# A dynamic convolution fused with a tanh-shrink MLP: softmax one superblock further ahead, three first products on GpSimd

## The chip, the cores and the metric

The kernel runs on one core of a Trainium2 chip. The metric is the device time of one execution in microseconds (us). Several executions are timed and their median is the time of the kernel. One further execution is taken with the hardware profiler, and every line of a profile below comes from such an execution. Times inside it count from the start of its span.

## The reference

```python
# x (8, 4096, 192), weight_gen (8, 4096, 8 heads, 7 taps)
w = exp(weight_gen - max); w = w / (sum(w, taps) + 1e-9)
out[b,s,h,g] = sum_k w[b,s,h,k] * x_pad[b, s+k, h*24+g]     # six rows of zeros ahead
h = out.reshape(32768, 192) @ w_in          # 192 -> 2048
y = (h - tanh(h)) @ w_out                   # 2048 -> 192, float32
```

Each token has its own softmax over seven taps for each of eight heads; the softmax weights multiply the token's row of x and the six rows before it. The result passes through two matmuls with `h - tanh(h)` between them.

## The kernel before

**Tiling.** The 32768 tokens are cut into 32 superblocks of 1024 tokens (`TOK`), numbered n. A partition holds eight neighbouring tokens. The 192 channels are cut into three chunks of 64 (`NC`), the 2048 hidden columns into sixteen f tiles of 128. Every PE operand uses 64 rows, and two row halves (r = 0, 1) stand side by side in the array.

**The stages of one superblock.**

- `load(n)` (L80) puts two transfers on SP's queue: `wg_t` with the weights (L84, 224 KB) and `x_t` with the rows of x (L93, 1344 KB; for the first superblock of a sequence a zero fill and three pieces, L103, L107, L93).
- `softmax_exp(n)` (L119) is one Exp on ACT.
- `softmax_norm(n)` (L129) is three instructions on DVE: the sum (`zsum`, L132), the reciprocal (L137), and the multiplication that gives `wsm` (L147). The reciprocal is written to the upper columns of a PSUM bank, here a bank of the second matmul (`obank`) or of the transposes (`pc`).
- `products(n)` (L153) multiplies the seven shifted copies of x with their tap's weight, 1536 elements a partition each, on GpSimd (POOL), except for the first two superblocks, where DVE takes some (`on_vector`). From superblock 3 on, a DMA adds the odd products onto the even ones (L179).
- `conv(n)` (L195) transposes the products on PE against an identity and sums them in PSUM (L213); ACT copies the sum to `convT` (L223).
- `gemm1(n, f)` (L240) is twelve half-array matmuls for two f tiles, six for one (L245), a Tanh on ACT (`th`, L255) and a subtraction on DVE (`gt`, L257).
- `gemm2(i)` (L264) is the second matmul for one block of 128 tokens (L277). Call i does the first half (r = 0) of block i and the second half of block i-1, in turns, in the banks `obank0` and `obank1`; ACT then copies block i-1 out (L295).

**The order.** The schedule is written out by hand (L362 to L403), and each engine runs its instructions in that order. The main loop runs over n, and inside it p runs from 0 to 7: two `gemm1` calls, from n = 1 on one `gemm2` call for the superblock before, and at fixed p the softmax of superblock n+3 and the transposes of superblock n+1. `products(n + 2)` is issued at the start of iteration n.

**What limits the queues.** The pool of `wg_t`, `e_t` and `wsm` has two buffers each, that of `x_t` two, that of the products two, and three PSUM buffers (`psum_h`) go round among `ph` and `pc`. So `gemm1` of f tile k waits until the `gt` of tile k-3 is done. The x of superblock n+3 can be loaded only when the products of superblock n+1 are finished on POOL.

**The start.** The weights w_in are loaded and cast by GpSimd's DMA queue in two parts: f tiles 0 to 5 (`load_w_in(0, FA)`) and the rest (`rest_of_w_in`, issued by the hook after product k = 2 of superblock 0). The upper 64 partitions get a copy of the lower ones, the first part on ACT's queue and the rest on SP's (L357). f tile 6 of superblock 0 needs that second copy.

Of the kernel before, what the change touches and what calls it, by code (L numbers as in the profile page):

```python
# [8 lines left out]
FP32 = mybir.dt.float32  # L9
BF16 = mybir.dt.bfloat16  # L10

ACT = mybir.ActivationFunctionType
# [4 lines left out]
def kernel(  # L17
# [8 lines left out]
    nc = tc.nc  # L26
# [24 lines left out]
    const = ctx.enter_context(tc.tile_pool(name="const", bufs=1))  # L51
    xpool = ctx.enter_context(tc.tile_pool(name="xpool", bufs=2))
    wgpool = ctx.enter_context(tc.tile_pool(name="wgpool", bufs=2))
    ppool = ctx.enter_context(tc.tile_pool(name="ppool", bufs=2))
    cpool = ctx.enter_context(tc.tile_pool(name="cpool", bufs=2))
    tpool = ctx.enter_context(tc.tile_pool(name="tpool", bufs=3))
# [20 lines left out]
    g1_act = {}  # L77
    last_wsm = {}

    def load(n):  # L80
        b, s = divmod(n, NSB)
        s0 = s * TOK
        wg_t = wgpool.tile([P, J, H, K], FP32, name="wg_t")
        nc.sync.dma_start(  # L84
            out=wg_t[:],
            in_=weight_gen[b, s0 : s0 + TOK].rearrange("(p j) h k -> p j h k", p=P),
        )

        x_t = xpool.tile([P, HALO + J, D], FP32, name="x_t")

        def rows(p0, p1):
            win = x[b, s0 + p0 * J - HALO : s0 + p0 * J - HALO + 1]
            nc.sync.dma_start(  # L93
                out=x_t[p0:p1, :, :],
                in_=bass.AP(
                    tensor=win.tensor,
                    offset=win.offset,
                    ap=[[J * D, p1 - p0], [D, HALO + J], [1, D]],
                ),
            )  # L100

        if s == 0:
            nc.sync.dma_start(  # L103
                out=x_t[0:1, 0:HALO, :],
                in_=zero[:].rearrange("o (h d) -> o h d", h=1).to_broadcast([1, HALO, D]),
            )
            nc.sync.dma_start(  # L107
                out=x_t[0:1, HALO : HALO + J, :],
                in_=x[b, 0:J].rearrange("(p j) d -> p j d", p=1),
            )  # L110

            rows(1, 16)
            rows(16, P)
        else:
            rows(0, P)
        wg_of[n] = wg_t
        x_of[n] = x_t

    def softmax_exp(n):  # L119
# [6 lines left out]
        )  # L126
        e_of[n] = e_t

    def softmax_norm(n, bank, in_psum=False):  # L129
        e_t = e_of.pop(n)  # L130
        zsum = wgpool.tile([P, J * H], FP32, name="zsum")
        nc.vector.reduce_sum(  # L132
            out=zsum[:], in_=e_t[:].rearrange("p j h k -> p (j h) k"), axis=AX.X
        )

        zr = bank[:, 512 - J * H : 512]
        nc.vector.reciprocal(zr, zsum[:])  # L137
        wsm_v = None
        if in_psum:
            wsm_v = obank[n % 2][:, 0 : J * H * K].rearrange("p (j h k) -> p j h k", j=J, h=H)  # L140
            scale(wsm_v, e_t, zr)
        wsm = wgpool.tile([P, J, H, K], FP32, name="wsm")
        last_wsm[0] = scale(wsm[:], e_t, zr)
        wsm_of[n] = (wsm, wsm_v)

    def scale(wsm, e_t, zr):
        return nc.vector.tensor_mul(  # L147
            wsm.rearrange("p j h k -> p (j h) k"),
            e_t[:].rearrange("p j h k -> p (j h) k"),
            zr.rearrange("p (n o) -> p n o", o=1).to_broadcast([P, J * H, K]),  # L150
        )

    def products(n, on_vector=(), hooks={}):  # L153
        x_t = x_of.pop(n)
        wsm, wsm_v = wsm_of.pop(n)
        in_pairs = n not in PLAIN

        even = ppool.tile([P, NPAIR, NC, J, H, GC], BF16, name="even")
        odd = ppool.tile([P, NPAIR, NC, J, H, GC], BF16, name="odd")
        last = ppool.tile([P, NC, J, H, GC], BF16, name="last")  # L160
        dst = {}
        for i in range(NPAIR):
            dst[2 * i] = even[:, i]
            dst[2 * i + 1] = odd[:, i]
        dst[K - 1] = last[:]
        if -1 in hooks:
            hooks[-1]()
        for k in range(K):
            eng, w = (nc.vector, wsm_v) if k in on_vector else (nc.gpsimd, wsm[:])
            eng.tensor_mul(  # L170
                dst[k].rearrange("p c j h g -> p j h c g"),
                x_t[:, k : k + J, :].rearrange("p j (h c g) -> p j h c g", h=H, c=NC),
                w[:, :, :, k : k + 1]
                .rearrange("p j h (k o) -> p j h k o", o=1)
                .to_broadcast([P, J, H, NC, GC]),
            )
            if k == K - 2 and in_pairs:

                nc.gpsimd.dma_start(  # L179
                    out=even[:].rearrange("p i c j h g -> p (i c j h g)")[:, 0:ACC],  # L180
                    in_=odd[:].rearrange("p i c j h g -> p (i c j h g)")[:, 0:ACC],
                    accum_op=mybir.AluOpType.add,
                    max_dma_last_dim=4096,
                )
            if k in hooks:
                hooks[k]()
        if in_pairs:
            groups = [even[:, i] for i in range(NPAIR)] + [last[:]]
            prods_of[n] = [
                groups + ([odd[:, NPAIR - 1]] if c == NC - 1 else []) for c in range(NC)  # L190
            ]
        else:
            prods_of[n] = [[dst[k] for k in sorted(range(K), key=lambda k: k in on_vector)]] * NC

    def conv(n, chunks):  # L195

        prods = prods_of[n]
        if n not in conv_of:
            conv_of[n] = cpool.tile([P, NC, HT], BF16, name="convT")
        convT = conv_of[n]  # L200
        nch = len(chunks)
        pc = psum_h.tile([P, 2, HT], FP32, name="pc", tag="ph")
        steps = [
            (gi, ci, c)
            for gi in range(max(len(prods[c]) for c in chunks))
            for ci, c in enumerate(chunks)
            if gi < len(prods[c])
        ]
        for si, (gi, ci, c) in enumerate(steps):
            for j in range(JH):  # L210
                col = (ci * JH + j) * R
                for r in range(2):
                    nc.tensor.matmul(  # L213
                        pc[:, r, col : col + R],
                        lhsT=prods[c][gi][r * R : (r + 1) * R, c, 2 * j : 2 * j + 2].rearrange(
                            "p j h g -> p (j h g)"
                        ),
                        rhs=ident[r * R : (r + 1) * R, r * R : (r + 1) * R],
                        start=(si == 0 and j == 0),
                        stop=(si == len(steps) - 1 and j == JH - 1),  # L220
                    )
        c0 = chunks[0]
        nc.scalar.activation(  # L223
            out=convT[:, c0 : c0 + nch, :].rearrange("p c (j r t) -> p r (c j) t", r=2, t=R),
            in_=pc[:, :, 0 : nch * JH * R].rearrange("p r (cj t) -> p r cj t", t=R),
            func=ACT.Copy,
        )
        if c0 + nch == NC:
            prods_of.pop(n)
        return pc[:, 0]  # L230

    def order(inst, other, reason):
        tc.add_manual_dep(
# [122 lines left out]
    def copy_w_in(f0, f1, eng):  # L356
        eng.dma_start(out=w_in[R:P, :, f0:f1], in_=w_in[0:R, :, f0:f1])  # L357
# [1 line left out]
    def rest_of_w_in():  # L359
        load_w_in(FA, F)  # L360

    load(0)  # L362
    softmax_exp(0)
    softmax_norm(0, obank[0], in_psum=True)
    load(1)
    load_w_in(0, FA)
    products(0, on_vector=(1, 3, 4, 5, 6), hooks={2: rest_of_w_in})
    softmax_exp(1)
    softmax_norm(1, obank[1], in_psum=True)
    copy_w_in(0, FA, nc.scalar)  # L370
    copy_w_in(FA, F, nc.sync)
    products(1, on_vector=(0, 1), hooks={4: load_w_out})
    conv(0, (0, 1))
    conv(0, (2,))
    load(2)
    for n in range(NTOT):
        if n + 3 < NTOT:
            load(n + 3)
        if 1 <= n < NTOT - 2:
            products(n + 2)  # L380
        for p in range(J):
            gemm1(n, 2 * p)
            gemm1(n, 2 * p + 1)
            if n == 0 and p == 1:
                softmax_exp(2)
            if p == 5 and n + 3 < NTOT:
                softmax_exp(n + 3)
            if n >= 1:
                gemm2((n - 1) * J + p)
            if n + 1 < NTOT:  # L390
                if p == (6 if n > 0 else 7):
                    conv(n + 1, (0, 1))
                if p == (6 if n > 1 else 7):
                    bank = conv(n + 1, (2,))
            if n == 0 and p == 1:
                softmax_norm(2, obank[0])
                products(2)
            if p == 6 and n + 3 < NTOT:

                softmax_norm(n + 3, bank if n > 1 else obank[0])  # L400
    gemm2(LAST)
    for j in range(J):
        gemm2_last(j)  # L403
# [30 lines left out]
```

The softmax here doesn't subtract the row's maximum and nothing guards it: scores larger than these inputs give would overflow.

## Time and profile before

| | us |
|---|---|
| median of 3 runs | 781.7 |
| lowest, highest | 778.25, 781.99 |
| the profiled execution | 779.38 |
| its span, first to last instruction | 777.4 |

| stage (from the timeline) | begins at us |
|---|---|
| `gemm1` of superblock 0 | 20.27 |
| transposes of superblock 1 | 43.97 |
| `gemm1` of superblock 1 | 48.08 |
| transposes of superblock 2 | 67.06 |
| transposes of superblock 3 | 91.78 |
| transposes of superblock 4 | 114.60 |
| transposes of superblock 5 | 137.42 |

The profiled execution's own time is 1.98 us above its span, and 2.32 us under the median. From superblock 3 on, one superblock takes 22.8 us in most iterations. The groups of instructions give the length of each operation: a `gt` on DVE 1.219 us, a Tanh on ACT 1.022, a product on POOL 2.962, an Exp 0.577, and the three instructions of a softmax on DVE 0.610, 0.561 and 0.622.

### The profile page before, as it was taken

The numbers are of one execution on the slowest core, as the hardware profiler recorded it, in microseconds if no ns is written. First come the engines' busy times: TensorE is split into PE (matmuls) and PEld (weight loads), VectorE is DVE, ScalarE is ACT, GpSimd is POOL, SyncE is SP. The second block draws the span as 40 slices with busy tenths as digits, with TensorE's granted clock in tenths as the row PEclk, the third lists the DMA queues.
The fourth block names the chain that finished last, engine by engine and source line by source line (L and its number), as shares of the span: only waits on it lengthen the run. The fifth ranks groups of instructions, "written<-read, shape, count | busy, mean of one in ns | idle before, by whom it ended". The sixth has DMA issues, their size and how long they took to land.

```text
span 777.4 us, 32332 instructions
## 1 busy us (share of the span) xinstructions
PE 742.6 (96%) x14784; PEld 582.8 (75%) x14784; DVE 671.3 (86%) x626; ACT 640.7 (82%) x865; POOL 664.4 (85%) x259
## 2 busy tenths in 40 slices
PE   2689999999999999999999999999999999999997
PEld 1257777777777778777777787777877777777777
DVE  6988898889889888989889898888898989888883
ACT  1678888888888888888888888888888888888883
POOL 5999999999989998999989989999899999998000
PEclk9899999999999999999999999999999999999999
DMA  7814676766545666454566544576544566633112
GB/s 203 201 63 106 160 180 179 178 167 158 118 141 140 180 180 178 89 141 144 169 180 160 137 119 146 159 180 180 155 87 150 149 180 179 167 78 77 44 43 83
DMA packets 25849, 111.38 MB, mean 143 GB/s; under 512 B 4801, under 2 KB 9841, under 8 KB 21625
## 3 DMA queue, kind: packets, MB, share of 16 engines
q1 hardware_dynamic: 14688, 77.04, 28.0%
q0 software_dynamic: 10816, 31.99, 25.2%
q8 instruction: 115, 1.88, 1.0%
q10 hardware_dynamic: 208, 0.29, 0.2%
q14 instruction: 22, 0.17, 0.1%
HBM read 54.49 MB, written 25.17 MB: 102 GB/s over the span
## 4 chain that ended last, share of the span: by engine, by line
PE 92%; DVE 2%; DMA 2%; issue 1%; ACT 1%; POOL 1%; SPq 0%; DVEq 0%; POOLq 0%
PE ph L245 43%; PE obank L277 42%; PE pc L213 6%; DVE gt L257 2%; PE po L311 1%; DMA w_in<-in_moe_w_in_dram 1%; DMA x_t<-in_x_dram 1%; DMA wg_t<-in_weight_gen_dram 1%; ACT th L255 1%; POOL even L170 1%; DVE wsm L147 0%; DVE obank L137 0%; DVE zsum L132 0%; POOL w_in L346 0%; SPq L103 0%
## 5 line engine op out<-in xcount | busy, mean ns | idle before, releaser
L257 DVE TENSOR_TENSOR gt<-ph,th 128x1024 bf16<-128x1024 f32 x512 | 602.8, 1219 | 68.7 <-ACT th L255 66.7
L255 ACT ACTIVATE th<-ph 128x1024 f32<-128x1024 f32 x512 | 497.0, 1022 | 68.2 <-PE ph L245 68.0
L245 PE MATMUL ph<-convT,w_in 64*128 64x512 bf16 x3072 | 388.8, 378 | 11.0 <-DVE gt L257 8.3
L277 PEld LDWEIGHTS <-gt 64*128 64x128 bf16 x7936 | 347.2, 94 | 52.6 <-issue 3.8
L277 PE MATMUL obank<-w_out,gt 64*128 64x192 bf16 x7936 | 376.8, 243 | 3.1 <-issue 1.8
L170 POOL TENSOR_TENSOR even<-x_t,wsm 128x1536 bf16<-128x1536 f32 x94 | 278.4, 2962 | 36.6 <-PE ph L245 29.6
L170 POOL TENSOR_TENSOR odd<-x_t,wsm 128x1536 bf16<-128x1536 f32 x92 | 272.5, 2962 | 0.0
L245 PEld LDWEIGHTS <-w_in 64*128 64x128 bf16 x3072 | 179.7, 94 | 120.3 <-issue 26.7
L170 POOL TENSOR_TENSOR last<-x_t,wsm 128x1536 bf16<-128x1536 f32 x31 | 103.4, 3337 | 0.0
L295 ACT ACTIVATE out_sb<-obank 128x192 f32<-128x192 f32 x248 | 82.2, 331 | 16.6 <-PE obank L277 11.5
L223 ACT ACTIVATE convT<-pc 128x1024 bf16<-128x1024 f32 x64 | 48.7, 808 | 30.1 <-PE pc L213 30.1
L213 PE MATMUL pc<-ident,even 64*128 64x64 bf16 x2304 | 48.3, 191 | 16.6 <-POOL even L170 15.1
L213 PEld LDWEIGHTS <-even 64*128 64x128 bf16 x2304 | 43.1, 96 | 17.3 <-POOL even L170 15.3
L179 POOL DMA_DIRECT2D even<-odd x29 | 34.9, 1205 | 9.0 <-POOL odd L170 9.0
L137 DVE RECIPROCAL pc<-zsum 128x64 f32<-128x64 f32 x27 | 15.1, 561 | 13.7 <-ACT convT L223 13.7
L122 ACT ACTIVATE e_t<-wg_t 128x448 f32<-128x448 f32 x32 | 18.5, 577 | 9.7 <-DMA wg_t<-in_weight_gen_dram 9.7
L213 PE MATMUL pc<-ident,last 64*128 64x64 bf16 x768 | 23.5, 191 | 0.3 <-DVE last L170 0.3
L132 DVE TENSOR_REDUCE zsum<-e_t 128x64 f32<-128x448 f32 x32 | 19.5, 610 | 4.1 <-ACT e_t L122 4.1
L147 DVE TENSOR_TENSOR wsm<-e_t,pc 128x448 f32<-128x448 f32 x27 | 16.8, 622 | 2.8
L213 PEld LDWEIGHTS <-last 64*128 64x128 bf16 x768 | 17.3, 96 | 0.4 <-DVE last L170 0.4
L213 PE MATMUL pc<-ident,odd 64*128 64x64 bf16 x448 | 15.6, 198 | 0.0
L213 PEld LDWEIGHTS <-odd 64*128 64x128 bf16 x448 | 11.5, 100 | 0.0
(20 smaller groups left out, 54.0 us busy)
## 6 DMA issues: line engine op xcount, KB each, us to landing
x_t<-in_x_dram SPq DMA_DIRECT2D x24, 1344.0 KB
even<-odd POOLq DMA_DIRECT2D x29, 1024.0 KB, 9.1
out_dram<-out_sb SPq DMA_DIRECT2D x31, 768.0 KB
x_t<-in_x_dram SPq DMA_DIRECT2D x8, 1176.0 KB
wg_t<-in_weight_gen_dram SPq DMA_DIRECT2D x32, 224.0 KB
x_t<-in_x_dram SPq DMA_DIRECT2D x8, 157.5 KB
w_out<-in_moe_w_out_dram POOLq DMA_DIRECT2D x1, 768.0 KB, 10.0
out_dram<-out_sb SPq DMA_DIRECT2D x4, 192.0 KB
```

Of the source, the lines that this page charges most:

```text
L122: nc.scalar.activation(out=e_t[:].rearrange("p j h k -> p (j h k)"), in_=wg_t[:].rearrange("p j h k -> p (j h k)"), func=ACT.Exp,)
L132: nc.vector.reduce_sum(out=zsum[:], in_=e_t[:].rearrange("p j h k -> p (j h) k"), axis=AX.X)
L147: return nc.vector.tensor_mul(wsm.rearrange("p j h k -> p (j h) k"), e_t[:].rearrange("p j h k -> p (j h) k"), zr.rearrange("p (n o) -> p ...
L170: eng.tensor_mul(dst[k].rearrange("p c j h g -> p j h c g"), x_t[:, k : k + J, :].rearrange("p j (h c g) -> p j h c g", h=H, c=NC), w[:, : ...
L179: nc.gpsimd.dma_start(out=even[:].rearrange("p i c j h g -> p (i c j h g)")[:, 0:ACC], in_=odd[:].rearrange("p i c j h g -> p (i c j h g)" ...
L213: nc.tensor.matmul(pc[:, r, col : col + R], lhsT=prods[c][gi][r * R : (r + 1) * R, c, 2 * j : 2 * j + 2].rearrange("p j h g -> p (j h g)") ...
L223: nc.scalar.activation(out=convT[:, c0 : c0 + nch, :].rearrange("p c (j r t) -> p r (c j) t", r=2, t=R), in_=pc[:, :, 0 : nch * JH * R].re ...
L245: nc.tensor.matmul(ph[:, r, :], lhsT=w_in[r * R : (r + 1) * R, c, f * P : (f + 1) * P], rhs=convT[r * R : (r + 1) * R, c, :], start=(c == ...
L255: last_act[0] = nc.scalar.activation(out=th[:], in_=ph_f, func=ACT.Tanh)
L257: nc.vector.tensor_sub(gt[:], ph_f, th[:])
L277: mm = nc.tensor.matmul(po[:, 0:D], lhsT=g_of[n][f][r * R : (r + 1) * R, col : col + P], rhs=w_out[r * R : (r + 1) * R, f, :], start=(r == ...
L295: last_act[0] = nc.scalar.activation(out=out_sb[:, j, :], in_=po[:, 0:D], func=ACT.Copy)
```

## The change

There are four parts.

1. The weights get their own load function (`load_wg`), and in the loop they are loaded for superblock n+4 instead of n+3, behind the x of superblock n+3. `wsm` moves to a pool of its own with three buffers. `softmax_exp` and `softmax_norm` run for superblock n+4 in iterations n >= 1. To get one superblock ahead, iteration 1 does two softmaxes: superblock 4 at p = 1 (Exp) and p = 2 (DVE), and superblock 5 at p = 5 and p = 7.
2. The weights of superblocks 2 and 3 are loaded before the second copy of w_in on SP's queue.
3. Of superblock 0, product k = 1 goes from DVE to GpSimd, which then does k = 0, 1, 2. The hook that loads the rest of w_in still stands after k = 2.
4. The last multiplication of superblock 2's softmax moves from DVE to GpSimd (`softmax_norm_gpsimd`), its place from p = 1 to p = 2. The transposes of superblock 0 are issued product by product over all three chunks, in the order 3, 0, 4, 5, 1, 6, 2, instead of chunks 0 and 1 first and then chunk 2.

```diff
+    wpool = ctx.enter_context(tc.tile_pool(name="wpool", bufs=3))
...
-    def load(n):
+    def load_wg(n):
         b, s = divmod(n, NSB)
         s0 = s * TOK
         wg_t = wgpool.tile([P, J, H, K], FP32, name="wg_t")
...
+        wg_of[n] = wg_t
+
+    def load_x(n):
+        b, s = divmod(n, NSB)
+        s0 = s * TOK
...
-    def softmax_norm(n, bank, in_psum=False):
+    def softmax_sum(n):
         e_t = e_of.pop(n)
         zsum = wgpool.tile([P, J * H], FP32, name="zsum")
         nc.vector.reduce_sum(
             out=zsum[:], in_=e_t[:].rearrange("p j h k -> p (j h) k"), axis=AX.X
         )
+        return e_t, zsum
+
+    def softmax_norm(n, bank, in_psum=False):
+        e_t, zsum = softmax_sum(n)
         zr = bank[:, 512 - J * H : 512]
         nc.vector.reciprocal(zr, zsum[:])
...
-        wsm = wgpool.tile([P, J, H, K], FP32, name="wsm")
-        last_wsm[0] = scale(wsm[:], e_t, zr)
+        wsm = wpool.tile([P, J, H, K], FP32, name="wsm")
+        last_wsm[0] = scale(nc.vector, wsm[:], e_t, zr)
         wsm_of[n] = (wsm, wsm_v)
 
+    def softmax_norm_gpsimd(n):
+        e_t, zsum = softmax_sum(n)
+        zr = wgpool.tile([P, J * H], FP32, name="zr")
+        nc.vector.reciprocal(zr[:], zsum[:])
+        wsm = wpool.tile([P, J, H, K], FP32, name="wsm")
+        scale(nc.gpsimd, wsm[:], e_t, zr[:])
+        wsm_of[n] = (wsm, None)
...
-            prods_of[n] = [[dst[k] for k in sorted(range(K), key=lambda k: k in on_vector)]] * NC
+            prods_of[n] = [[dst[k] for k in (sums or range(K))]] * NC
...
-    def conv(n, chunks):
+    def conv(n, *parts):
...
+        pcs = [psum_h.tile([P, 2, HT], FP32, name="pc", tag="ph") for _ in parts]
+        for gi in range(max(len(g) for g in prods)):
+            for chunks, pc in zip(parts, pcs):
...
-    load(0)
+    load_wg(0)
+    load_x(0)
     softmax_exp(0)
     softmax_norm(0, obank[0], in_psum=True)
-    load(1)
+    load_wg(1)
+    load_x(1)
     load_w_in(0, FA)
-    products(0, on_vector=(1, 3, 4, 5, 6), hooks={2: rest_of_w_in})
+    products(
+        0,
+        on_vector=(3, 4, 5, 6),
+        sums=(3, 0, 4, 5, 1, 6, 2),
+        hooks={2: rest_of_w_in},
+    )
     softmax_exp(1)
     softmax_norm(1, obank[1], in_psum=True)
+    load_wg(2)
+    load_wg(3)
     copy_w_in(0, FA, nc.scalar)
     copy_w_in(FA, F, nc.sync)
     products(1, on_vector=(0, 1), hooks={4: load_w_out})
-    conv(0, (0, 1))
-    conv(0, (2,))
-    load(2)
+    conv(0, (0, 1), (2,))
+    load_x(2)
     for n in range(NTOT):
         if n + 3 < NTOT:
-            load(n + 3)
+            load_x(n + 3)
+        if n + 4 < NTOT:
+            load_wg(n + 4)
         if 1 <= n < NTOT - 2:
             products(n + 2)
         for p in range(J):
             gemm1(n, 2 * p)
             gemm1(n, 2 * p + 1)
-            if n == 0 and p == 1:
-                softmax_exp(2)
-            if p == 5 and n + 3 < NTOT:
-                softmax_exp(n + 3)
+            if n <= 1 and p == 1:
+                softmax_exp(2 * n + 2)
+            if p == 5 and n + 3 + (n > 0) < NTOT:
+                softmax_exp(n + 3 + (n > 0))
             if n >= 1:
                 gemm2((n - 1) * J + p)
             if n + 1 < NTOT:
                 if p == (6 if n > 0 else 7):
                     conv(n + 1, (0, 1))
                 if p == (6 if n > 1 else 7):
                     bank = conv(n + 1, (2,))
-            if n == 0 and p == 1:
-                softmax_norm(2, obank[0])
+            if n == 0 and p == 2:
+                softmax_norm_gpsimd(2)
                 products(2)
-            if p == 6 and n + 3 < NTOT:
-                softmax_norm(n + 3, bank if n > 1 else obank[0])
+            if n == 1 and p == 2:
+                softmax_norm(4, obank[0])
+            if n == 0 and p == 6:
+                softmax_norm(3, obank[0])
+            if n > 0 and p == (6 if n > 1 else 7) and n + 4 < NTOT:
+                softmax_norm(n + 4, bank)
```

## The prediction

> **What bounds the kernel now.** I read the page's engine shares first, then the chain of work that ended last, then busy time by stage, then the chain and the timeline of the first 75 us, where nearly all of the change lies.
>
> ```profile
> span 777.4 us, 32332 instructions
> PE 92%; DVE 2%; DMA 2%; issue 1%; ACT 1%; POOL 1%; SPq 0%; DVEq 0%; POOLq 0%
> 0.00:20.20 20.20, 4.77 (x166) 4.46 (x168) 12.86 (x14) 3.46 (x4) 10.04 (x14) 1.00 0.76 202
> 20.20:44.00 23.80, 15.20 (x109) 6.10 (x105) 22.00 (x21) 16.43 (x19) 23.16 (x9) 0.86 0.82 209
> 114.60:137.40 22.80, 22.77 (x468) 17.83 (x461) 20.45 (x20) 19.91 (x28) 22.50 (x9) 1.00 0.60 154
> ```
>
> After the span and the chain's shares come stages: start and end, length, then busy time of PE, weight load, DVE, ACT and POOL, granted clock, DMA share and GB/s. In a steady superblock PE is busy 22.77 of 22.80 us. The softmax there lies beside the transposes and costs nothing, so moving it a superblock earlier can gain nothing there. Only the first two superblocks have idle PE to win.
>
> The chain from 15 us in order of time, then lines of the timeline (start, length, instruction, idle time before it and its releaser):
>
> ```profile
> 15.64 1.13 POOL w_in L346 x2
> 16.77 7.11 DMA w_in<-in_moe_w_in_dram
> 24.02 0.71 SPq L357
> 24.84 4.33 DMA wg_t<-in_weight_gen_dram
> 28.65 0.52 PEld L245 LDWEIGHTS <-w_in 64*128 64x128 bf16 x6 [0.61 <-DMA w_in<-w_in]
> 32.93 5.94 PE L245 MATMUL ph<-convT,w_in 64*128 64x512 bf16 x30 [3.46 <-DVE gt L257]
> 34.00:37.50 3.50, 3.50 (x18) 1.51 (x17) 3.10 (x4) 2.56 (x3) 3.50 (x2) 0.50 1.41 182
> 45.68 2.35 DVE L257 TENSOR_TENSOR gt<-ph,th 128x1024 bf16<-128x1024 f32 x2
> 57.90 1.56 PE L277 MATMUL obank<-w_out,gt 64*128 64x192 bf16 x32
> 55.97 2.36 DVE L257 TENSOR_TENSOR gt<-ph,th 128x1024 bf16<-128x1024 f32 x2 [0.90 <-ACT th L255]
> 58.58 2.36 DVE L257 TENSOR_TENSOR gt<-ph,th 128x1024 bf16<-128x1024 f32 x2 [0.26 <-ACT th L255]
> 58.58 0.36 SPq L84 DMA_DIRECT2D wg_t<-in_weight_gen_dram  x1
> 64.58 0.58 ACT L122 ACTIVATE e_t<-wg_t 128x448 f32<-128x448 f32 x1
> 65.20:67.30 2.10, 2.10 (x51) 1.97 (x47) 1.84 (x2) 2.10 (x3) 2.10 (x1) 1.00 0.04 5
> 70.75 1.48 PE L277 MATMUL obank<-w_out,gt 64*128 64x192 bf16 x31 [0.43 <-DVE wsm L147]
> ```
>
> The reader is to see three things. The rest of w_in leaves POOL at 15.64, its copy on SP follows at 24.02, the weights of superblock 2 queue behind it, and PE stands 3.46 us until DVE has done that softmax. In superblock 1 DVE has only 0.26 us of slack per pair of `gt`. And where the second matmul shares its bank with a softmax (70.75), PE waits for `wsm`.
>
> [...] after the 3.46 us gap the clock is 0.50 until about 37.9. [...] So weights issued behind an x load come behind it; the weights issued at 58.58 behind the x pieces agree, with packets until about 67.2. [...]
>
> **Part by part.**
>
> Third product on GpSimd. POOL starts at 9.93 and a product comes every 2.86 us (20.82 to 23.69), so the third ends at 18.5, and the issue of the rest of w_in moves from 15.64 to 18.5. From that issue to SP's copy took 8.4 us, from the copy to f tile 6 another 4.6. Unchanged, tile 6 starts at 31.5. The 8.4 has a tail in which the DMA share is 0.06 (22 to 24), so it may be 2 us shorter: bounds 29.5 and 31.5; I take 30.7. DVE has one product fewer (1.7 us), so its first `gt` can start at 22.4 instead of 23.99; the last transposes follow the third product at 18.6 and end near 19.5, so `gemm1` starts at 20.3 to 20.4 as before. Tiles 0 to 5 then end near 29.3 and wait for w_in: the earlier start is lost there. The transposes' new order only keeps the start level: without it, the 56 of chunk 2 (18.72 to 20.45) would all follow those of chunks 0 and 1, some 1.3 us more behind the late product.
>
> Weights of superblocks 2 and 3 ahead of the copy. This takes the softmax of superblock 2 off the path; its sum and reciprocal lie in the w_in wait. What is late next is tile 6. From tile start to `gt` took 1.93 us at full clock (25.26 to 27.2) and 2.56 at half (32.93 to 35.49). The gap before tile 6, 27.0 to 30.7, should again halve the clock, so `gt6` starts at 33.2. Then eight `gt` at 1.15 (4.61 for four), the softmax of superblock 3 (43.83 to 45.68, 1.85) and two `gt` (2.35) end at 46.6; with 0.2 for slow tiles (1.28 apart, not 1.15) 46.8. Before it was 45.68 + 2.35 = 48.03. Gain 1.2; with tile 6 at 29.5 or 31.5 it is 2.4 or 0.4. The 224 KB loads end before w_in's second part starts, so I cost them nothing; uncovered they would delay w_in by 1 us each.
>
> Scale on GpSimd. 448/1536 of 2.962 is 0.86[...]. I take 0.9. Products of superblock 1 can start at 20.3 (POOL free) instead of 20.82, so POOL ends superblock 2 0.4 us later than before. The transposes waiting for it have over 7 us to spare, so this costs nothing there; but the x and weight loads of superblocks 4 and 5 follow 0.4 later.
>
> Softmax of superblock 4 at p = 2 of iteration 1. It stands between `gt5` and `gt6`, writes `obank0`, and `gemm2(3)`, whose second matmul goes to that bank, must wait for its `wsm`. Everything behind it on PE waits too, for `gemm1` of tiles 8 and 9 comes next. In before's clock `gt5` ends at 58.33, a softmax adds 1.9, so `gemm2(3)` starts at 60.2 instead of 57.90: 2.3 us. The trace never shows this wait in this place. Lower bound 1.5, if only the DVE delay over its 0.26 slack counts; upper 2.4. I take 2.3. Nothing hides it, since PE is bound there.
>
> Softmax of superblock 5. Its weights are now issued behind the x of superblock 4, which waits for POOL, and its Exp comes in the same iteration, where the one of superblock 4 stood (64.58). With -1.2 + 2.3 it is due at 65.7. The weights' bulk landed by 65.2, single packets until 67.2; plus 0.4 gives 65.6 to 67.6. ACT's copy before `gemm2(6)` (65.05 + 0.33 against 65.74) leaves 0.36 slack. PE loses 0 to 1.5; I take 0.8. Its DVE part at p = 7 delays the third tile pair by about as much as the wait at 70.75 (0.43, with its start 0.67) took, which goes: together -0.2, between -0.3 and +0.5.
>
> Steady superblocks. The weights still come in the iteration that uses them. In iteration 2 the DMA share falls from 0.95 (84 to 88) over 0.58 to 0.06 (90 to 92), so x and weights are there by 90; Exp is due at 89.06 + 1.7 = 90.8. Later there is more room. Queue SP's output copy stands behind the x load as before. I cost this at nothing; without cover it would be about 1 us a superblock.
>
> Sum: -1.2 + 2.3 + 0.8 - 0.2 = +1.7. The profiled execution took 779.38, so 781.1 for such a run. The median of before is 2.3 above the profiled one; the same distance gives 783.4.
>
> **Rivals.** The likeliest case is this sum: 783.4, its own range 781 to 785.5. A floor backs it: Exp of superblock 5 can't start before its weights, so even with the best start PE stands 65.6 - 64.58 - 0.36 = 0.7 us behind before at that point.
>
> Clock drop in superblock 1 (the slower side): [...] For it: one gap of 3.46 us did so. Against: the 2.42 us gap before 25.26 didn't. The drop seen lasted from 31.1 to 37.9, 6.8 us; at half rate half of it is lost, 3.4, less the 0.8 wait it hides: +4.3, or 786.0. It decides from about 6 us of slow clock on.
>
> Late weights in every early superblock, until POOL runs ahead (it first waits for PE at 187): one us in six superblocks on top of 1.7, less the overlap, 789. For it: transfers of x, sums and output keep the DMA busy until 90. Against: Exp comes 13 us after the x issue later on (121.25 to 134.70).
>
> The start gain survives: tile 6 at 29.5 and `gemm2(3)` not held (the bank's columns are different ones). Then -2.4 - 0.2, or 779.1. Against: before's 70.75 shows just this wait, and the floor has to fall too: POOL would have to be 3 us earlier for the weights to be there by 62.5.
>
> **Numbers.** Under 0.5% (3.9 us) the measurement can't tell from no change. Chances: likeliest sum 0.70, clock drop 0.17, late weights 0.08, gain survives 0.05. Slower by over 0.5% comes from half of the clock drop, the late weights and the upper tail of the sum: 0.27; faster only from scatter around the last rival: 0.05; the rest 0.68. Before's own runs spread 3.7 us, so the range is 779.5 to 788.
>
> **What would show it.** A w_in wait of PE at tile 6 near 30 us with no wait for the weights there; transposes of superblock 1 about 1 us earlier than 43.97; a wait of PE on DVE `wsm` of about 2.3 us near 59; an Exp on ACT waiting for `wg_t` near 66; transposes of superblock 3 about 1.7 us later than 91.78, and 22.8 us a superblock from there. If `gemm2(3)` doesn't wait, or the weights of superblock 5 land before 65, the sum is wrong on the high side; a clock of 0.50 after 59, or Exp waits in iterations 2 and on, make it too low.

## The result and the profile after

| | before | after |
|---|---|---|
| median of 4 runs, us | 779.98 | 829.77 |
| lowest, highest | 778.13, 781.99 | 825.24, 834.29 |
| span of the profiled execution | 777.4 | 832.5 |

The ratio after to before is 1.0638, with a 95% interval from 1.0563 to 1.0713. The change makes the kernel 6.4% slower; the forecast was 783.4 us. Before has one run more here than ahead of the prediction, 778.13 us, which moves its median from 781.7 to 779.98. The profiled execution of after took 834.29 us.

The first two lines to read are again the span and the engines' shares of the chain that ended last, here of after.

```profile
span 832.5 us, 32339 instructions
PE 83%; issue 6%; POOL 5%; DVE 2%; DMA 2%; ACT 1%; SPq 0%; DVEq 0%; POOLq 0%; ACTq 0%
```

Before, PE held 92% of the chain and "issue" 1%. "Issue" is time in which an engine waited for nothing that the profile shows. Now it holds 6%, some 50 us against some 8, most of the 55 us by which the span grew. POOL's 5% lies in the first 57 us, where the chain now runs through its products. So most of the loss isn't an engine that became slower, and it isn't a wait for data that the profile names.

The start is not where it lies. These are lines of after's timeline (start, length, instruction, idle time before it and its releaser), in the places that the forecast named.

```profile
29.25 2.11 PE L261 MATMUL ph<-convT,w_in 64*128 64x512 bf16 x17 [0.94 <-DMA w_in<-w_in]
40.41 0.41 PE L228 MATMUL pc<-ident,even 64*128 64x64 bf16 x16 [0.31 <-DVE gt L273]
56.73 1.51 PE L293 MATMUL obank<-w_out,gt 64*128 64x192 bf16 x31 [2.15 <-DVE wsm L164]
66.47 0.58 ACT L127 ACTIVATE e_t<-wg_t 128x448 f32<-128x448 f32 x1 [1.35 <-DMA wg_t<-in_weight_gen_dram]
92.96 0.88 PE L228 MATMUL pc<-ident,even 64*128 64x64 bf16 x48
```

The reader sees PE's wait for w_in at f tile 6, the transposes of superblock 1 3.56 us earlier than before's 43.97, the wait of `gemm2(3)` for `wsm`, the Exp of superblock 5 waiting for its weights, and the transposes of superblock 3 1.36 us later than before's 91.60 on this view. From there a superblock takes 22.8 us until the transposes at 207.06: about 1.4 us are lost in the first quarter of the run, against the 1.7 of the forecast.

The rest is lost later. These are four lines of after's list of waits (who waited for whom, us in total, times, longest).

```profile
POOL even L187 <- PE pc L228: 82.7, 22, 7.9
PE obank L293 <- issue: 18.3, 7, 3.3
PE pc L228 <- issue: 13.5, 9, 4.0
PE ph L261 <- issue: 10.2, 4, 4.0
```

And two of before's list:

```profile
POOL even L170 <- PE ph L245: 29.6, 21, 2.3
PE obank L277 <- issue: 1.8, 3, 0.9
```

PE stops on "issue" for 42 us in after, in pieces of up to 4 us, in all three kinds of matmul. Before has 1.8 us in the row shown. POOL's wait changes its releaser too: before it starts a new superblock's products some time after the transposes, after it starts right behind them.

One such stop, by short stretches of after: start and end, length, then busy time of PE, weight load, DVE, ACT and POOL, granted clock, DMA share, GB/s.

```profile
207.00:209.00 2.00, 1.98 (x113) 1.76 (x110) 2.00 (x3) 1.37 (x3) 1.49 (x2) 1.00 1.06 188
211.00:212.00 1.00, 1.00 (x18) 0.59 (x14) 1.00 (x2) 0.90 (x2) 1.00 (x2) 1.00 1.01 165
212.00:214.00 2.00, 0.00 (x0) 0.00 (x0) 1.31 (x2) 0.00 (x0) 2.00 (x1) 1.00 0.93 371
217.00:218.00 1.00, 1.00 (x12) 0.71 (x10) 0.90 (x1) 0.33 (x1) 1.00 (x2) 0.50 0.00 0
```

The transposes (most of the 113 matmuls in 2 us) run at 207 to 209 with the DMA full. At 212 to 214 PE starts not one matmul and not one weight load, and the DMA is still full. Then comes a stretch at half clock, so one stop is paid twice. The timeline of after around these transposes shows what stands beside them.

```profile
203.96 1.20 POOL L196 DMA_DIRECT2D even<-odd  x1 [0.30 <-POOL odd L187]
207.06 0.88 PE L228 MATMUL pc<-ident,even 64*128 64x64 bf16 x48
208.12 0.33 SPq L99 DMA_DIRECT2D x_t<-in_x_dram  x1
208.60 2.90 POOL L187 TENSOR_TENSOR even<-x_t,wsm 128x1536 bf16<-128x1536 f32 x1 [0.51 <-PE pc L228]
214.06 1.04 PE L261 MATMUL ph<-convT,w_in 64*128 64x512 bf16 x8 [2.06 <-issue]
```

The same transposes in before's timeline:

```profile
204.50 1.20 POOL L179 DMA_DIRECT2D even<-odd  x1 [0.30 <-POOL odd L170]
205.71 0.88 PE L213 MATMUL pc<-ident,even 64*128 64x64 bf16 x48
209.07 0.62 DVE L147 TENSOR_TENSOR wsm<-e_t,pc 128x448 f32<-128x448 f32 x1
209.83 2.90 POOL L170 TENSOR_TENSOR even<-x_t,wsm 128x1536 bf16<-128x1536 f32 x1 [1.18 <-PE ph L245]
```

Before, POOL's first product of a superblock starts at 209.83, 0.14 us after the `wsm` that it needs is done (209.07 + 0.62 = 209.69), and 4.1 us after the transposes began. The releaser that the profile names, PE, had ended the transposes 2.3 us earlier (207.41). After the change that `wsm` has been ready for a whole superblock, so the product starts at 208.60, 1.5 us after the transposes began. Softmax had been pacing POOL. Taking it away lets POOL's products come 2.6 us earlier against PE, and with them what POOL triggers: the transfer that adds the odd products onto the even ones (1024 KB, "the summing transfer" below) is issued 3.1 us ahead of the transposes instead of 1.2. It gets there step by step, since POOL needs less time for a superblock than PE: in after 21.56 us from one summing transfer's issue to the next between 139.28 and 203.96, while a steady superblock takes 22.8. Counted from the records of the DMA packets, the first packet of that transfer comes so many us after the transposes begin, at the transposes of superblocks 4 to 10:

```
before     +4.4   +3.2   +1.9   +0.6   +0.6   -0.2   +0.6
after      +3.7   +2.5   +1.2   -0.1   -1.3   -5.7   -1.7
```

Before, the drift ends at +0.6, held there by `wsm`. After the change it runs on, and at -1.3 comes the first long stop, the one above.

**What stops PE.** The trace also records transfers of instructions: queue q8, in the page's third part (packets, MB, share) `q8 instruction: 115, 1.88, 0.9%`, so 16 KB each. That they bring PE's is read from the stops, which end 1.2 to 1.6 us after one of them has landed (below). PE has 29568 instructions (14784 matmuls and as many weight loads) and 35 of its sequencer, some 257 for each packet; that a packet is a block of 256 the period of the stops shows below. Around the transposes above (counted from the records of instructions and DMA packets, as are the listings below; "asked for" is an estimate: the earliest point in a block at which any packet of after begins, the 175th instruction):

```
us                             before                after
transposes begin               205.71                207.06
summing transfer, packets      206.28 to 213.12      205.72 to 212.30
next block asked for           205.92                207.26
its packet begins, ends        208.60, 209.55        211.79, 212.90
PE stands still                210.65 to 211.01      212.00 to 214.06
```

Before, the packet waits 2.7 us, and PE stops for 0.36. After, it waits 4.5 us, until the summing transfer is nearly through. PE runs on what it still has, stops, and starts again 1.2 us after the packet is in. Every one of the 17 stops over 0.7 us between 100 us and the last `gemm1` of after begins at the same number of PE's stream modulo 256, which is 193 (counted from 0, with the sequencer's own instructions, one a superblock from superblock 3 on). Every one ends 1.2 to 1.6 us after a packet of q8 has landed. Together they take 40.7 us. A steady superblock has 913 of these instructions, so the program has no period of 256; the fetch has.

### The profile page after: what moved, and what is told of

Same layout as the page of the kernel before. It is cut to its first block, busy times and chain, and to the rows that moved or that the text cites. A ratio compares the mean times of both kernels' runs of the same rounds, so it can differ in the third digit from the quotient of the medians.

```text
span 832.5 us, 32339 instructions
## 1 busy us (share of the span) xinstructions
PE 759.4 (91%) x14784; PEld 595.2 (71%) x14784; DVE 668.5 (80%) x624; ACT 642.1 (77%) x865; POOL 668.1 (80%) x261
## 3 DMA queue, kind: packets, MB, share of 16 engines
q8 instruction: 115, 1.88, 0.9%
## 4 chain that ended last, share of the span: by engine, by line
PE 83%; issue 6%; POOL 5%; DVE 2%; DMA 2%; ACT 1%; SPq 0%; DVEq 0%; POOLq 0%; ACTq 0%
PE obank L293 39%; PE ph L261 38%; PE pc L228 5%; POOL even L187 2%; POOL odd L187 2%; PE po L327 1%; DVE gt L273 1%; ACT convT L239 1%; DMA wg_t<-in_weight_gen_dram 1%; DMA x_t<-in_x_dram 1%; DVE pc L146 0%; POOL last L187 0%; DVE wsm L164 0%; ACT th L271 0%; POOL w_in L362 0%
## 5 line engine op out<-in xcount | busy, mean ns | idle before, releaser
L261 PE MATMUL ph<-convT,w_in 64*128 64x512 bf16 x3072 | 396.2, 385 | 17.9 <-issue 10.2
L293 PEld LDWEIGHTS <-gt 64*128 64x128 bf16 x7936 | 355.7, 96 | 74.5 <-issue 26.6
L293 PE MATMUL obank<-w_out,gt 64*128 64x192 bf16 x7936 | 386.4, 246 | 22.2 <-issue 18.3
L187 POOL TENSOR_TENSOR odd<-x_t,wsm 128x1536 bf16<-128x1536 f32 x93 | 277.7, 2986 | 1.5 <-PE pc L228 1.5
L261 PEld LDWEIGHTS <-w_in 64*128 64x128 bf16 x3072 | 182.8, 96 | 127.3 <-issue 34.2
L228 PEld LDWEIGHTS <-even 64*128 64x128 bf16 x2304 | 42.9, 96 | 10.6 <-issue 8.7
L137 DVE TENSOR_REDUCE zsum<-e_t 128x64 f32<-128x448 f32 x32 | 19.5, 608 | 2.9 <-ACT e_t L127 2.9
```

What stands on the lines that cost most here:

```text
L137: nc.vector.reduce_sum(out=zsum[:], in_=e_t[:].rearrange("p j h k -> p (j h) k"), axis=AX.X)
L187: eng.tensor_mul(dst[k].rearrange("p c j h g -> p j h c g"), x_t[:, k : k + J, :].rearrange("p j (h c g) -> p j h c g", h=H, c=NC), w[:, : ...
L228: nc.tensor.matmul(pc[:, r, col : col + R], lhsT=prods[c][gi][r * R : (r + 1) * R, c, 2 * j : 2 * j + 2].rearrange("p j h g -> p (j h g)") ...
L261: nc.tensor.matmul(ph[:, r, :], lhsT=w_in[r * R : (r + 1) * R, c, f * P : (f + 1) * P], rhs=convT[r * R : (r + 1) * R, c, :], start=(c == ...
L293: mm = nc.tensor.matmul(po[:, 0:D], lhsT=g_of[n][f][r * R : (r + 1) * R, col : col + P], rhs=w_out[r * R : (r + 1) * R, f, :], start=(r == ...
```

## The experiments

The theories, once this was seen. The first (A): the summing transfer lies badly against the transposes. Its rivals: the weights of superblock n+4, now ahead of the output copy on SP's queue, are in the way; or something else in the change, such as the new start, costs the time. Ratios are to the kernel before in the same comparison, with 95% intervals; they are the recorded ones, from which the quotient of the two medians can differ by 0.4%. Each sum of stops holds 0.4 us ahead of the last `gemm2`, which is a wait for ACT:

| kernel | median us | ratio to before | PE stops over 0.3 us after 100 us, sum |
|---|---|---|---|
| before | 779 to 782 | 1 | 3.3 |
| the change | 829.77 | 1.0638 [1.0563, 1.0713] | 42.2 |
| e1_hold_pool | 788.98 | 1.0105 [1.0041, 1.0168] | 6.8 |
| e2_weights_after_out | 828.77 | 1.0594 [1.0535, 1.0654] | 40.0 |
| e3_new_start_only | 782.02 | 1.0015 [0.9993, 1.0037] | 8.1 |
| e4_late_sum | 822.95 | 1.0523 [1.0464, 1.0581] | 32.5 |
| e5_start_hold_gt15 | 771.89 | 0.9887 [0.9834, 0.9940] | 1.0 |
| e6_start_hold_gt1 | 772.46 | 0.9894 [0.9842, 0.9947] | 0.9 |
| e7_start_hold_gt5 | 792.69 | 1.0147 [1.0089, 1.0206] | 19.5 |
| e8_change_hold_gt1 | 777.09 | 0.9949 [0.9932, 0.9965] | 0.8 |
| e9_before_hold_gt15 | 774.79 | 0.9921 [0.9896, 0.9947] | 0.4 |
| e10_change_hold_gt15 | 776.76 | 0.9942 [0.9924, 0.9961] | 0.4 |

**e1: the change, but POOL waits again.** The first product of superblock n+2 waits for the `wsm` of superblock n+3, which the new program computes at the time at which before computed that of n+2.

```diff
-    def products(n, on_vector=(), sums=None, hooks={}):
+    def products(n, on_vector=(), sums=None, hooks={}, hold=None):
-            eng.tensor_mul(
+            inst = eng.tensor_mul(
+            if k == 0 and hold is not None:
+                order(inst, hold, "products after the next softmax")
-            products(n + 2)
+            products(n + 2, hold=last_wsm[0])
```

> The changed kernel with one wait more: the first product of superblock n+2 on GpSimd also waits for the wsm of superblock n+3, which DVE finishes right after the transposes of superblock n, so GpSimd starts its products where it did before the change. Theory A (GpSimd is no longer held by the softmax, so its summing DMA comes 2.6 us earlier against the transposes and blocks PE's instruction fetch): the idle PE of 2 to 4 us marked issue goes, 22.8 us a superblock, about 781.5 us (780 to 784). Theory B (the weights' new place behind x on SP's queue crowds the DMA): nothing changes, 825 to 834 us.

788.98 us: one wait added gives back 41 of the 50 us. That is what theory A says, though the time lands some us above its figure. POOL's row in the list of waits of e1 is again like before's:

```profile
POOL even L187 <- PE ph L263: 35.5, 23, 3.0
PE obank L295 <- issue: 5.4, 8, 1.6
```

The rest of the excess is four stops over 0.7 us, of 0.8 to 1.6 us (4.3 us together), all at number 193. In the superblocks with stops the summing transfer's packets begin between 0.6 us after the transposes and 1.2 us before them: before's own timing stands at the edge.

**e2: the weights behind the output copy.**

```diff
-        if n + 4 < NTOT:
-            load_wg(n + 4)
+        if n == 0:
+            load_wg(4)
...
                 gemm2((n - 1) * J + p)
+                if p == 0 and n + 4 < NTOT:
+                    load_wg(n + 4)
```

> The changed kernel with the weights of superblock n+4 issued behind the output copy of iteration n, as they came before the change, instead of directly behind x. Theory A: GpSimd's timing is the same, so 822 to 836 us. Theory B (place of the weights): about 782 us, with idle PE gone after 200 us; 1 or 2 us may come on top where an Exp of the first iterations waits for its weights.

828.77 us, within the spread of the change itself. The place of the weights is out as a cause.

**e3: the change's start with before's softmax order.** The start's parts (third product on POOL, weights of superblocks 2 and 3 first, scale on POOL, order of the transposes) stay. The softmax of n+3 goes back to p = 5 and p = 6 of iteration n.

```diff
-            if n <= 1 and p == 1:
-                softmax_exp(2 * n + 2)
-            if p == 5 and n + 3 + (n > 0) < NTOT:
-                softmax_exp(n + 3 + (n > 0))
+            if n == 0 and p == 1:
+                softmax_exp(2)
+            if p == 5 and n + 3 < NTOT:
+                softmax_exp(n + 3)
...
-            if n == 1 and p == 2:
-                softmax_norm(4, obank[0])
-            if n == 0 and p == 6:
-                softmax_norm(3, obank[0])
-            if n > 0 and p == (6 if n > 1 else 7) and n + 4 < NTOT:
-                softmax_norm(n + 4, bank)
+            if p == 6 and n + 3 < NTOT:
+                softmax_norm(n + 3, bank if n > 1 else obank[0])
```

> The changed kernel's start (weights 2 and 3 early, third product and scale on GpSimd, transposes product by product) with the softmax of superblock n+3 at p = 5 and 6 as before the change. Theory A: GpSimd waits for wsm again, no idle PE after 200 us, and the 3.5 us won before the transposes of superblock 1 stay: 776 to 778 us, faster than before. Theory C (what the start moved, through GpSimd and the DMA queues, is what the later superblocks pay for): 800 us or more.

A miss: 782.02, no measurable difference from before, where 776 to 778 us was expected. The transposes of superblock 3 do start 2.3 us earlier (89.28 against 91.60), but five stops of together 6.2 us come later, against two of 1.7 us in before. Before, e1 and e3 all stop for over 0.3 us in superblocks 11, 15, 18 and 22, where the packets come 0.6 us after the transposes as in many others that don't stop. So it seems to depend on where blocks end, and on tenths of a us of phase: at this edge what a gain at the start is worth is luck. And the start's parts are out as the cause of the 50 us.

**e4: the change with the summing transfer after the last product.** If the place of the summing transfer alone decides, putting it behind the seventh product should end most stops.

```diff
-            if k == K - 2 and in_pairs:
+            if k == K - 1 and in_pairs:
```

> The changed kernel with the summing DMA issued after the seventh product instead of the sixth, some 3.4 us later; nothing else moves, x even comes earlier. Theory A (the summing DMA's place against the transposes is what counts): its packets begin some 1 us after the transposes begin, as before the change, and the idle PE is gone or nearly so: 781 to 790 us. Theory B, or any theory in which x or the weights hold PE's instruction fetch: still 820 us or more.

822.95 us, where 781 to 790 was expected: A in this simple form falls. The timeline of e4 shows why.

```profile
205.85 1.15 POOL L196 DMA_DIRECT2D even<-odd  x1
205.93 0.33 SPq L99 DMA_DIRECT2D x_t<-in_x_dram  x1
207.10 0.88 PE L228 MATMUL pc<-ident,even 64*128 64x64 bf16 x48
214.27 1.83 PE L261 MATMUL ph<-convT,w_in 64*128 64x512 bf16 x8 [2.23 <-issue]
```

```
e4, us
x load, packets                206.88 to 213.38
summing transfer, packets      211.42 to 218.70
next block asked for           207.30
its packet begins, ends        211.92, 212.80
```

Both transfers are now issued together when POOL finishes, and the x load is the one that is running when the transposes come. The stop is the same, 2.23 us. So it isn't the accumulation and not POOL's queue: **theory A, refined**: whichever large transfer runs while the transposes' next block is asked for holds that block back, in e4 by 4.6 us (207.30 to 211.92).

**e5 to e8: where the transfers do no harm.** By the refined theory the phase decides. In e5 and e6 (on e3's order) the first product of n+2 waits for a `gt` that DVE finishes after the transposes: the last one of superblock n-1 as issued, or `gt1` of superblock n. In e7 it waits for `gt5`, so that the summing transfer comes far behind the transposes, but the x load comes shortly ahead of the next ones. e8 is the whole change with e6's wait. e5's edit, on top of e3:

```diff
+            if k == 0 and hold is not None:
+                order(inst, hold, "phase of the products")
...
-        nc.vector.tensor_sub(gt[:], ph_f, th[:])
+        last_gt[0] = nc.vector.tensor_sub(gt[:], ph_f, th[:])
...
-            products(n + 2)
+            products(n + 2, hold=last_gt[0])
```

In the other three, the call itself moves into the loop over p, behind the two `gemm1` calls (p == 0 for e6 and e8, p == 2 for e7):

```diff
+            if 1 <= n < NTOT - 2 and p == 0:
+                products(n + 2, hold=last_gt[0])
```

> The start-only version with one wait more: the first product of superblock n+2 waits for the last gt of superblock n-1, some 2 us later than the wsm it waits for anyway. Refined theory A (PE stops where its next 256 instructions are asked for while the transposes, which use up some 340 instructions in 1.5 us, run under a DMA burst; the burst is the summing DMA with the x load behind it): the burst now begins 2 to 3 us after the transposes begin instead of 0.6, so fewer idle PE stretches than in the kernel before: 774 to 779 us. Rival (GpSimd being held at all costs time, or its phase doesn't matter): 782 us or more.

> The same with the wait for gt 1 of superblock n, some 4.5 us later than wsm. Refined theory A: the burst of 14 us begins about 5 us after the transposes begin and is over before the next ones: 773 to 778 us, no idle PE over 1 us after 200 us. Rival (a later GpSimd only costs): 784 us or more, with PE waiting for products.

> The same with the wait for gt 5 of superblock n, some 10 us later than wsm. The sums should now begin about 10 us after the transposes and the x load lie under the next transposes. Refined theory A: idle PE marked issue comes back, 790 to 825 us. Rival (only too early a GpSimd hurts): as with gt 1, below 780 us.

> The changed kernel as it is, all four parts, with the products of superblock n+2 waiting for gt 1 of superblock n. Refined theory A: the whole loss was the phase of GpSimd's transfers, so 775 to 781 us; some 1.4 us more than the start-only version with this wait, for the two softmaxes of superblock 1. Rival (the softmax a superblock ahead costs something of its own in the steady superblocks): over 790 us.

(The expectation of e5 speaks of some 340 instructions in the transposes. Counted, they are 208 from superblock 3 on, 104 matmuls and 104 weight loads, in 1.5 us.)

e5 took 771.89, e6 772.46, e8 777.09: all three faster than before, e5 by 1.1%. e5 and e6 came out below their ranges, so the phase was worth more than expected; and e8 lies 4.6 us above e6, not 1.4, which is taken up below. The page of e5:

```profile
span 770.1 us, 32338 instructions
PE 92%; DVE 3%; ACT 1%; DMA 1%; POOL 1%; issue 1%; SPq 0%; DVEq 0%; POOLq 0%
```

Its timeline, at the transposes of the same superblock as above:

```profile
203.72 0.88 PE L231 MATMUL pc<-ident,even 64*128 64x64 bf16 x48
204.72 1.20 POOL L199 DMA_DIRECT2D even<-odd  x1 [0.30 <-POOL odd L188]
210.04 2.90 POOL L188 TENSOR_TENSOR even<-x_t,wsm 128x1536 bf16<-128x1536 f32 x1 [1.18 <-DVE gt L276]
```

And that superblock as one stretch, with the columns as above:

```profile
203.72:226.54 22.82, 22.79 (x461) 17.86 (x458) 20.46 (x20) 19.93 (x28) 21.34 (x9) 1.00 0.61 154
```

The summing transfer is issued 1.0 us after the transposes begin (after the change: 3.1 us before), its packets start 2.8 us after them, and the DMA moves as much as ever (154 GB/s). From the transposes at 158 us on, every superblock but the last takes 22.82 us. The wait costs POOL 1.18 us a superblock, which nobody misses.

e7 took 792.69, slower than before by 1.5%. A row of its list of waits:

```profile
PE pc L231 <- issue: 18.6, 15, 2.1
```

And its timeline within the transposes that begin at 228.74:

```profile
228.82 0.80 PE L231 MATMUL pc<-ident,even 64*128 64x64 bf16 x43
231.59 0.29 PE L231 MATMUL pc<-ident,even 64*128 64x64 bf16 x8 [1.50 <-issue]
```

```
e7, us
x load, packets                222.64 to 228.69
next block asked for           225.55
its packet begins, ends        229.31, 230.28
```

Here the summing transfer (packets 10.6 us behind the transposes) is far away, and the x load, 6 us ahead of them, holds the block back by 3.8 us. 80 of the 104 transposes run, then PE stands 1.5 us in their midst. e5 delays POOL a little and wins; e7 delays it more and loses. A theory in which an earlier POOL is bad as such can't give both; the refined theory does.

**e9 and e10: the wait alone.** e9 is before with e5's wait and nothing else, e10 the whole change with it. The edit is e5's.

> The kernel before, with only the one wait added: the first product of superblock n+2 on GpSimd also waits for the last gt of superblock n-1. Refined theory A: the idle stretches of PE that the kernel before has after 100 us go, while its start stays: 774 to 777 us, 2.5 to 5 us above the start-only version with this wait, which took 771.9. Rival (the gain of that version came from the start alone): 780 us.

> The changed kernel, all four parts, with that same wait. Refined theory A: steady superblocks of 22.8 us as in the start-only version; what is left between the two (771.9 there) are the two softmaxes of superblock 1 with PE waiting for wsm and ACT for the weights: 775 to 778 us. Rival (the softmax a superblock ahead costs more than that): over 780 us.

e9 took 774.79, e10 776.76. So one wait takes 53 us off the change and 6 off before (780.91 in that comparison). Of the 6, stops over 0.3 us make up 2.9 in the profiled executions, whose spans differ by 4.0; the rest wasn't taken apart. e10's page:

```profile
span 774.9 us, 32318 instructions
PE 90%; DVE 3%; POOL 2%; DMA 2%; issue 1%; ACT 1%; SPq 0%; DVEq 0%; POOLq 0%; ACTq 0%
```

The two programs of e10 and after differ in that wait only, so their difference is the price of the phase: 832.5 - 774.9 = 57.6 us of span. It is the stops over 0.7 us, 40.7, plus the time that PE's matmuls take longer at half clock: its busy time is 759.4 us in after and 741.6 in e10, 17.8. Together 58.5, which is the price to within 1 us. The clock's own records agree: after has eleven stretches of 3.41 us at 0.50 inside its span, half of which is 18.8 us, and e10 has none before its last 1.2 us.

Of these kernels e5 is the best: the change's start, before's softmax order, and the wait.

## Why the prediction was right and wrong

**Start gain, -1.2: the mechanism held, the size was too small.** The transposes of superblock 1 came 3.56 us earlier. Of the 2.4 us that it is off, 1.45 are the DMA tail before SP's copy of w_in: tile 6 started at 29.25, not 30.7, just under the lower bound of 29.5. Another 0.63 is the clock: the forecast let the gap before tile 6 halve it, but that gap was 0.94 us and the clock stayed at 1.00, so `gt6` followed 1.93 us after its tile, not 2.56.

**Wait of `gemm2(3)`, +2.3**: 2.15 measured. **Exp of superblock 5, +0.8**: the Exp waited 1.35 at 66.47, and PE 0.91 behind it (first line below). **Scale on POOL, 0.9**: it took 0.97. The transposes of superblock 3 came 1.36 later, against +1.7. The early part was right as a sum although two terms were off by some 2 us: the start gained 3.56, not 1.2, and superblocks 1 and 2 lost 3.56 + 1.36 = 4.92, not 2.3 + 0.8 - 0.2 = 2.9. That they offset each other isn't chance alone; it is the forecast's own floor. PE goes on only when ACT has copied behind the Exp of superblock 5, and its weights land at 66.45, in the forecast's 65.6 to 67.6. They come behind the x that is issued ahead of them: counted from after's packets, that x runs from 59.30 to 65.15, the weights from 64.31 to 65.93. What the start gains ahead of that, PE waits there. The first line is of after, the second of e10, which has no half clock there:

```profile
67.32 1.50 PE L293 MATMUL obank<-w_out,gt 64*128 64x192 bf16 x32 [0.91 <-ACT out_sb L311]
68.96 1.50 PE L296 MATMUL obank<-w_out,gt 64*128 64x192 bf16 x32 [3.36 <-ACT out_sb L314]
```

Without stops the two terms are seen apart: e5 against e9 (the start alone) is 771.89 - 774.79 = -2.9 us, e10 against e5 (the softmaxes) +4.9. In e10 PE waits 2.15 us for `gemm2(3)` and 3.36 behind that Exp, so the Exp was the term priced too low. The sum of the two differences, e10 against e9, is +2.0 against the forecast's +1.7, though their ranges overlap and the sign isn't certain.

**"Steady superblocks ... I cost this at nothing": this is the step that failed.** The question put there was whether weights and x arrive in time, and they do. In its place the runs show 57.6 us, the span of after above that of e10. Two things were missed.

First, POOL's wait was read by the releaser that the profile names: the forecast says that POOL "first waits for PE at 187". The timeline of before says otherwise: 209.83 against a `wsm` done at 209.69, and at 187.01 against one done at 186.87. That wait was POOL's pace, and the change removes it. So an edit that was costed as moving a softmax earlier in fact moved two transfers of more than 1 MB a superblock. The forecast's list of what is moved had the DMAs of SP, but not the summing transfer, which no line of the diff touches.

Second, PE's instruction supply wasn't counted among the resources. The page shows it (q8), with 0.9% of the DMA's time, and it looks like nothing. Of a resource that is needed at one moment, the share says little.

**"Clock drop in superblock 1"**: it came, behind the wait of `gemm2(3)` at p = 2 (2.15 us), and was short: 3.41 us at 0.50 from 58.05 on, which costs up to half of that, 1.7 us, where the rival had 3.4. It isn't why superblocks 1 and 2 lost more than the forecast: e10 has the same wait of 2.15 us, keeps its full clock, and loses 5.7 us there (transposes of superblock 1 at 41.27, of 3 at 94.60). Half clock became a large cost only later, behind the stops, which no rival had. **"Late weights in every early superblock"**: no. The Exp waits of after are three in all. **The range**: its upper end, 788, came from costs at the start. A cost per superblock stood in the text as "about 1 us a superblock" without cover (224 KB at the 209 GB/s of its stage from 20.20 to 44.00 would be 1.1, by estimate); over the 29 superblocks from 3 on that would have reached 812 (783.4 + 29), and what came was twice as much: 1.4 us of stops and 0.6 of half clock (40.7 and 17.8 over 29).

**The fetch and its queue.** The traces show a period of 256 instructions (every one of the 17 long stops of after begins at number 193), and in e5, e8, e9 and e10 no stop of PE over 0.7 us; in after such stops take 40.7 us. Single packets of q8 begin 4.5 us (after, 211.79) and 6.7 us (before, 216.53) after they are asked for, by the estimate above, while the summing transfer or an x load runs. How the DMA engines divided their time between the queues then, no run shows.

**What stays open.** A kernel with other instruction counts on PE, so that blocks end elsewhere, wasn't tried; nor was one without the summing transfer. So that a different place of the block's end would move the stops is argued, not shown; that before, e1 and e3 stop in the same four superblocks speaks for it. In e10 the two waits of 2.15 and 3.36 us are 0.6 us more than the +4.9; where that went wasn't taken apart.

## What to carry to other kernels

Before a wait is removed, ask what else it paced: list every transfer that the released engine issues or frees, and see where each will fall against the stretches in which PE takes many instructions in a short time. Where PE stands on "issue" for whole microseconds, look for large transfers in the 6 us before and count its instructions modulo 256. One ordering edge that puts a transfer behind the dense stretch can be worth more than the work it delays.

## What the runs showed of the hardware

- **PE's reserve of instructions.** In after a block's packet begins no earlier than at the 175th instruction of the block before (in the other traces the earliest is the 165th, in e7), and PE stops at number 193 of the next one: by estimate some 274 instructions of reserve. In the ordinary part of a superblock PE takes (913 - 208) / (22.82 - 1.52) = 33.1 a us, so by estimate the reserve lasts some 8.3 us; where all of the transposes' 208 in 1.5 us fall into it, some 3.5, and at the stop shown 4.7 (207.26 to 212.00). A block is usable after its delay, 0.95 us for the packet (median of after's 115), and 1.2 to 1.6 us more. Held back 4.9 us in e5 (207.80 to 212.70), away from the transposes, it comes in time; held back 4.5 us in after, under them, it doesn't.
- **The same number in every trace looked at.** After 100 us, all stops over 0.3 us but the one ahead of the last `gemm2` begin at 193. Over 0.7 us they are 17 in after, 17 in e2, 13 in e4, 11 in e7, 5 in e3, 4 in e1, 2 in before; e5, e6, e8, e9 and e10 have none. All 69 end 1.2 to 1.6 us after a packet of q8 has landed.
- **It feeds itself.** In after, a stop delays PE but not POOL, so in the next superblock the summing transfer begins up to 7.6 us ahead of the transposes (5.7 the first time), and the x load behind it is the one in the way. The superblocks of after alternate: 26.53, 24.44, 27.82, 24.53, 27.75 us.
- **Half clock: idle time within one window.** After's records of the granted clock lie on a grid: its eleven stretches at 0.50 last 3.41 us each and begin whole multiples of 3.41 us apart. Counted in windows of this grid, PE was idle 2.06 us or more ahead of each of the eleven, and 1.98 at most in those windows at full clock that no drop followed; over all twelve traces, from 22 us on, the least ahead of a drop is 1.92 us, the most without one 2.01. So in these traces it isn't the length of a gap that decides but how much of it lies in one window: the gap of 2.42 us that the forecast named (before 25.26, in before) and those of 2.15 and 3.36 us in e10 fall across two windows, with at most 1.8 us idle in either, and the clock stayed at 1.00. That of 2.06 us ahead of 214.06 lies in one.
